# Bits by plain float32 matmuls on the raw head, one V-product block per head, one byte offset for all tiles

## The chip, the cores and the metric

The kernel runs on one core of a Trainium2 chip. The metric is the device time of one execution in microseconds (us), the median of several runs. The profile shows one more execution, instruction by instruction.

## The reference

Attention over 16 heads (2 batches of 8) of 768 tokens by 64, in which a query sees only the keys whose six sign bits against a random projection equal its own, and then two dense layers in a row:

```python
q_bits = (np.einsum('bhsd,dk->bhsk', q, proj) > 0)      # and k_bits; proj is 64 x 6
mask = q_bucket[:, :, :, None] == k_bucket[:, :, None, :]
scores = np.where(mask, scale * np.matmul(q, k.transpose(0, 1, 3, 2)), -1000000000.0)
attn = softmax(scores); x = np.matmul(attn, v)          # 1536 tokens x 512
h = np.maximum(np.maximum(x @ w1, x @ w2), x @ w3) @ w_out
h2 = h @ w_in; g = (h2 + 1)**2 / 4, 0 below -1, h2 above 1
out = g @ w_out2
```

## The kernel before

Two stages follow each other on the tensor engine: the attention of all heads, and the MLP, a long run of 128x512 matmuls. Float32 accuracy comes from pairs of rounded parts (hi, lo, type float32r) and three matmuls per product.

A head has six query tiles of 128 rows, 96 tiles in all. For a tile the tensor engine makes the scores in a bank pair s_ps (four matmuls over 384 keys: L374 with lo and qa, L377 with hi and qb, for each half of the keys), VectorE takes the minimum with a cap and the row's extreme (t_max, L384), ScalarE the exponential (t_exp, L396), the tensor engine transposes the result in six pieces (t_tr, L404, banks t_ps0 and t_ps1), and ScalarE or VectorE copies these into pt (t_out, L413). Three tiles make a group, half a head. Its product with V (g_pv, L422) is six plain float32 matmuls with 64 weight columns; they come in pairs, one into partitions 0 to 63 of the bank u_ps and one into 64 to 127. ScalarE copies the bank out (g_copy, L436 and L439), and SyncE (SP) moves one half beside the other (g_fold: L447 for even heads, one DMA a group; L449 and L450 for odd heads, two). In the text a T is the six transposes of a tile, and a QK its four score matmuls.

The bits of a head enter the score matmul as 12 more rows of qb and hi (rows 64 to 75), as large numbers that push a pair with unequal bits to the cap. bits_mm (L337) makes the projections of half a head by three float32r matmuls with 108 weight columns into pj_ps; the first half is thresholded by VectorE (bits_now, L344), the second by ScalarE and GpSimd (bits_sign L351, bits_rows L359). One DMA (prep_move "kb", L329, hi<-qb) then carries the key's bits from qb to hi. Every QK of that head waits for it.

The raw head r (L272) is scaled and split by GpSimd and moved by further DMAs on SP. All DMAs of the stage stand in SP's one queue, in a fixed order.

That order, and the order on every other engine, comes from a small planner (class Work): each task has an engine, a cost, a due number and what it comes after; the planner replays them at build time and emits each when its turn comes. Its costs are written by hand (for a fold 0.15 us on SP, for a PV group 2.0 us on the tensor engine).

SBUF tiles lie one behind the other, so the byte at which a tile starts within its partition follows from the sizes before it. Counted from a multiple of 256 bytes, before the change ident, x_hl, w and the weight staging start at 0; two small tiles (sums, 48 bytes in two buffers) shift all that follows, so hi, lo, qa, qb, p, pt, vr, and in the MLP wx, hh and g start at 128. The MLP's weights lie in w (five slices of seven) or wx (two of seven).

Of the kernel before, what the change touches and what calls it, by code (L numbers as in the profile page):

```python
# [8 lines left out]
F32 = mybir.dt.float32  # L9
F32R = mybir.dt.float32r  # L10
# [100 lines left out]
def lsh_attention_moe_kernel(  # L111
# [28 lines left out]
    pj_raw = const.tile([128, 108], F32, name="pj_raw")  # L140
    pj_st = const.tile([128, 2, 108], F32R, name="pj_st")
# [107 lines left out]
    def attention(mlp_steps):  # L249
        with ExitStack() as ax, ExitStack() as sx:  # L250
# [4 lines left out]
            pt_p = ax.enter_context(tc.tile_pool(name="pt", bufs=2))  # L255
# [86 lines left out]
            def bits_now(h, half, bank):  # L342
                rows = slice(64, 108)
                nc.vector.tensor_scalar(  # L344
                    out=head[h]["qb"][rows, half * HALF:(half + 1) * HALF], in0=bank[rows, 0:HALF],
                    scalar1=pc_sb[rows, 0:1], scalar2=pc_sb[rows, 1:2], op0=ALU.is_gt, op1=ALU.mult,
                )

            def bits_sign(h, half, bank):
                z = sm_p.tile([128, HALF], F32, tag="z", name="z", bufs=1)  # L350
                nc.scalar.activation(  # L351
                    out=z[64:108], in_=bank[64:108, 0:HALF], func=ACTF.Sign, scale=HUGE, bias=pc_sb[64:108, 2:3]
                )
                head[h]["z", half] = z

            def bits_rows(h, half, eng):
                z = head[h]["z", half]
                rows = slice(64, 108)
                eng.tensor_scalar(  # L359
                    out=head[h]["qb"][rows, half * HALF:(half + 1) * HALF], in0=z[rows],  # L360
                    scalar1=pc_sb[rows, 3:4], scalar2=pc_sb[rows, 3:4], op0=ALU.mult, op1=ALU.add,
                )
# [68 lines left out]
            def g_copy(g):  # L431
                pr, cs = g_cut(g)
                if g % 4 < 2:
                    if g % 4 == 0:
                        pr["u"] = nm_p.tile([128, S], F32, tag="u", name="u")
                    nc.scalar.copy(out=pr["u"][:, cs], in_=u_ps[:, 0:HALF])  # L436
# [83 lines left out]
            pj_split()  # L520
# [35 lines left out]
            def head_tasks(h):
                due = NK * h - 9
                hp, rp = place("prep", NK), place("r", 3)
# [14 lines left out]
                mms, rows = [], []  # L573
                for half in range(2):
                    bp = place("pj", 1)
                    mms.append(task("PE", 0.52, due + 2, bits_mm, h, half, pj_ps, after=[hi] + lo, takes=[bp]))
                    if half == 0:
                        rows.append(task("DVE", 0.72, due + 2, bits_now, h, half, pj_ps, after=[mms[-1]], leaves=[bp]))
                    else:
                        zp = place("z", 1)  # L580
                        sg = task("ACT", 0.69, due + 2, bits_sign, h, half, pj_ps, after=[mms[-1]], takes=[zp], leaves=[bp])
                        rows.append(task("POOL", 0.75, due + 2, bits_rows, h, half, nc.gpsimd, after=[sg], leaves=[zp]))
                kh = task("SP", 0.1, due + 2, prep_move, h, "kh", after=mms + [move["ql"]], lag=3.5)
                kb = task("SP", 0.1, due + 1, prep_move, h, "kb", after=mms + rows + [move["qa"], move["qb"]], lag=2.5)
                ready[h] = [kh, kb, move["qa"], move["ql"]]
# [328 lines left out]
```

## Time and profile before

| | us |
|---|---|
| median of 3 runs (704.96 to 705.01) | 704.96 |
| the profiled execution | 704.98 |
| its span, first to last instruction | 703.2 |
| tensor engine busy | 695.2 |

The profiled execution lies 0.02 us from the median, so sums made on it hold for the median too. 1.8 us lie outside the span. A matmul's row in the profile lasts longer than its turn, since matmuls overlap in the array; the turn is read from the start of one row to the start of the next.

### The profile page before, as it was taken

To read this page: it belongs to the slowest core of one execution; us is meant where nothing else is said; L and a number is where in the kernel's file an instruction comes from. 1 tells how busy PE (TensorE), PEld (TensorE's weight loads), DVE (VectorE), ACT (ScalarE), POOL (GpSimd) and SP (SyncE) were. 2 spreads that over 40 slices of the span, in tenths; PEclk is the share of its full clock that TensorE was granted. 3 is DMA by queue.
4 is the path that set the end of the run, shared out by engine and by line. 5 is a ranking of instruction groups with operands and counts; after the bars stand their busy time and mean duration, and the time that the engine had idled before them with its cause. 6 is when DMAs were issued, how large, how long until landed. Compare 5 with 4: busy or idle time off the path is not lost.

```text
span 703.2 us, 9982 instructions
## 1 busy us (share of the span) xinstructions
PE 695.2 (99%) x3548; PEld 553.9 (79%) x3548; DVE 455.5 (65%) x696; ACT 374.0 (53%) x733; POOL 282.7 (40%) x262
## 2 busy tenths in 40 slices
PE   8999999999999999999999999999999999999998
PEld 6777777777777688888888888888888888888886
DVE  6646555666655486775444355765888888888844
ACT  4788898888888423332321233665544444444430
POOL 3555646647523034442332022444344344344330
PEclk9999999999999999999999999999999999999999
DMA  5655557546511222221111022120111122111004
GB/s 164 162 149 151 132 145 202 139 121 167 132 46 45 95 91 90 90 91 52 56 49 54 31 89 90 47 75 31 60 61 61 60 66 84 61 61 60 31 0 180
DMA packets 25658, 62.78 MB, mean 89 GB/s; under 512 B 4085, under 2 KB 9813, under 8 KB 25609
## 3 DMA queue, kind: packets, MB, share of 16 engines
q1 hardware_dynamic: 25576, 62.15, 29.2%
q8 instruction: 28, 0.46, 0.3%
q14 instruction: 22, 0.17, 0.1%
q0 software_dynamic: 32, 0.00, 0.0%
HBM read 42.07 MB, written 3.19 MB: 64 GB/s over the span
## 4 chain that ended last, share of the span: by engine, by line
PE 97%; DVE 1%; issue 0%; DMA 0%; ACT 0%; DVEq 0%; ACTq 0%
PE b L708 47%; PE b L835 19%; PE u_ps L422 10%; PE t_ps L404 9%; PE s_ps L374 5%; PE s_ps L377 5%; PE pj_ps L337 2%; DMA r<-in_kq 0%; DVE p L384 0%; DVE lo L302 0%; DVE qb L344 0%; DVE qa L331 0%; DVE pt L413 0%; PE pj_ps L469 0%; ACT pt L413 0%
## 5 line engine op out<-in xcount | busy, mean ns | idle before, releaser
L708 PE MATMUL b<-x_hl,w 128*128 128x512 f32 (+1 forms) x900 | 203.1, 382 | 0.0
L708 PEld LDWEIGHTS b<-x_hl,w 128*128 128x128 f32 x900 | 164.0, 188 | 34.2 <-issue 0.6
L384 DVE TENSOR_SCALAR_CACHE_REDUCE p<-s_ps 128x768 f32<-128x768 f32 x96 | 91.1, 955 | 43.7 <-PE s_ps L377 32.4
L735 POOL TENSOR_TENSOR g<-r,g 128x512 fp32r<-128x512 f32 x48 | 62.6, 1306 | 125.6 <-ACT g L734 125.6
L835 PE MATMUL b<-w,g 128*128 128x512 f32 (+1 forms) x438 | 108.4, 392 | 0.0
L219 POOL TENSOR_TENSOR w<-wg,w 128x512 fp32r<-128x512 f32 (+1 forms) x42 | 59.4, 1414 | 96.7 <-ACT w L213 80.8
L835 PEld LDWEIGHTS b<-w,g 128*128 128x128 f32 x438 | 81.9, 189 | 18.7
L396 ACT ACTIVATE p<-p,nm 128x768 f32<-128x768 f32 x96 | 89.8, 937 | 9.0 <-DVE p L384 8.5
L192 DVE SCALAR_TENSOR_TENSOR wg<-wg,wr 128x512 f32<-128x512 f32 (+1 forms) x58 | 66.1, 1140 | 36.2 <-ACT wg L190 35.4
L213 ACT CAST w<-wg 128x512 fp32r<-128x512 f32 (+1 forms) x42 | 25.4, 605 | 115.6 <-DVE wg L205 115.6
L708 PE MATMUL b<-x_hl,wx 128*128 128x512 f32 x360 | 86.1, 395 | 0.0
L404 PEld LDWEIGHTS t_ps<-ident,p 128*128 128x128 f32 x576 | 66.5, 140 | 22.7 <-ACT p L396 11.5
L404 PE MATMUL t_ps<-ident,p 128*128 128x128 f32 x576 | 82.1, 276 | 1.1 <-DVE pt L413 0.9
L708 PEld LDWEIGHTS b<-x_hl,wx 128*128 128x128 f32 x360 | 67.9, 189 | 15.8
L413 ACT COPY pt<-t_ps 128x384 f32<-128x384 f32 x158 | 69.5, 480 | 18.2 <-PE t_ps L404 16.3
L374 PE MATMUL s_ps<-lo,qa 128*128 128x384 f32 x192 | 72.3, 377 | 1.0 <-DVE p L384 0.9
L422 PE MATMUL u_ps<-pt,vr 128*64 128x384 f32 x384 | 69.6, 495 | 0.2 <-ACT pt L413 0.2
L377 PE MATMUL s_ps<-hi,qb 76*128 76x384 f32 x192 | 65.3, 340 | 0.2 <-DVE hi L331 0.2
L815 DVE SCALAR_TENSOR_TENSOR r<-r,b 128x512 f32<-128x512 f32 x48 | 33.0, 687 | 48.2 <-ACT r L814 47.8
L842 DVE TENSOR_TENSOR acc<-b,acc 128x512 f32<-128x512 f32 (+1 forms) x85 | 56.5, 676 | 8.0 <-PE b L835 8.0
L813 ACT ACTIVATE r<-b,half_sb 128x512 f32<-128x512 f32 x48 | 32.9, 686 | 46.1 <-PE b L708 40.8
L197 DVE TENSOR_SCALAR wg<-wg 128x512 int32<-128x512 int32 (+1 forms) x58 | 53.9, 929 | 2.8
(80 smaller groups left out, 847.5 us busy)
## 6 DMA issues: line engine op xcount, KB each, us to landing
wr<-in_w SPq DMA_DIRECT2D x50, 512.0 KB, 3.1
r<-in_kq SPq DMA_DIRECT2D x15, 384.0 KB, 3.9
vr<-in_v SPq DMA_DIRECT2D x16, 192.0 KB
rb<-d SPq DMA_DIRECT2D x16, 192.0 KB, 3.3
wr<-in_w SPq DMA_DIRECT2D x8, 384.0 KB, 2.8
qa<-hi SPq DMA_DIRECT2D x15, 192.0 KB
qb<-hi SPq DMA_DIRECT2D x15, 192.0 KB, 4.0
qa<-lo SPq DMA_DIRECT2D x15, 192.0 KB, 2.7
```

Source lines behind the costliest of these rows:

```text
L192: nc.vector.scalar_tensor_tensor(out=f32(g), in0=f32(g), scalar=TINY_SQ, in1=f32(high), op0=ALU.is_ge, op1=ALU.mult)
L219: nc.gpsimd.tensor_tensor(out=w[:, 1, 0:cols], in0=f32(g2), in1=f32(w[:, 0, 0:cols]), op=ALU.subtract)
L374: nc.tensor.matmul(out=o, lhsT=hd["qa"][:, qs], rhs=hd["lo"][:, ks], start=True, stop=False)
L377: nc.tensor.matmul(out=o, lhsT=hd["qb"][0:76, qs], rhs=hd["hi"][0:76, ks], start=False, stop=True)
L384: nc.vector.tensor_scalar(out=p.rearrange("p (a k) -> p a k", a=2), in0=s_ps[n % 2][:, :, 0:HALF], scalar1=MASKED, scalar2=MASKED, op0=ALU ...
L396: nc.scalar.activation(out=p, in_=p, func=ACTF.Exp, scale=-1.0, bias=tl[n]["nm"], accum_out=pair[h // 2]["sums"][:, c:c + 1],)
L404: nc.tensor.transpose(out=t_ps[half][:, j * 128:(j + 1) * 128], in_=tl[n]["p"][:, kt * 128:(kt + 1) * 128], identity=ident,)
L413: copy(out=grp[g][:, 3 * half:3 * half + 3, r * 128:(r + 1) * 128], in_=t_ps[half][:, 0:HALF].rearrange("p (j q) -> p j q", j=3),)
L422: nc.tensor.matmul(out=u_ps[rows, 0:HALF], lhsT=vr[:, kt, :], rhs=grp[g][:, kt, :], start=(i == 0), stop=(i == 2),)
L708: nc.tensor.matmul(out=outp, lhsT=w_[a], rhs=x_[b_], start=(i == 0 and jj == 0), stop=(i == n - 1 and jj == 2),)
L735: nc.gpsimd.tensor_tensor(out=dst[:, 1, cs], in0=src, in1=f32(dst[:, 0, cs]), op=ALU.subtract)
L835: nc.tensor.matmul(out=pb[:, cs], lhsT=gs[f][:, a, tsl], rhs=wt[:, b_, cs], start=(n == 0), stop=(n == len(terms) - 1),)
```

## The change

The bits of a head are now made from the raw head r, before the split, by one plain float32 matmul per half with 64 weight columns (pj_sc for heads 0 and 1, pj_raw for the others, whose r is scaled in place). The two halves go to the two partition halves of pj_ps, and VectorE thresholds both in one operation (bits_rows, L350 after). The result z is carried by four DMAs (bits_move, L357 after): two into qb, two into hi. For heads 2 to 15 these matmuls stand at the head of a block: bits of head h + 2, then both PV groups of head h, the first into u_ps and the second into pj_ps. So a head has one PV block and not two. pt has four buffers. pj_raw, pj_sc and sums take 256 bytes each, and every tile behind them starts at byte 224 of 256.

```diff
--- before.py
+++ after.py
-    pj_raw = const.tile([128, 108], F32, name="pj_raw")
-    pj_st = const.tile([128, 2, 108], F32R, name="pj_st")
+    pj_raw = const.tile([128, 64], F32, name="pj_raw")
+    pj_sc = const.tile([128, 64], F32, name="pj_sc")
...
-            pt_p = ax.enter_context(tc.tile_pool(name="pt", bufs=2))
+            pt_p = ax.enter_context(tc.tile_pool(name="pt", bufs=4))
...
-                for c0 in (64, 96):
+                for c0 in (0, 32):
                     nc.gpsimd.tensor_scalar(
                         out=pj_raw[:, c0:c0 + 6], in0=pj_raw[:, c0:c0 + 6], scalar1=-1.0, scalar2=0.0, op0=ALU.mult, op1=ALU.add
                     )
-
-            def pj_split():
-                nc.scalar.copy(out=pj_st[:, 0, :], in_=pj_raw)
-                nc.vector.tensor_tensor(out=pj_st[:, 1, :], in0=pj_raw, in1=f32(pj_st[:, 0, :]), op=ALU.subtract)
+                nc.gpsimd.tensor_scalar(
+                    out=pj_sc, in0=pj_raw, scalar1=sc_sb, scalar2=0.0, op0=ALU.mult, op1=ALU.add
+                )
...
-            def bits_mm(h, half, bank):
-                hd = head[h]
-                cs = slice(half * HALF, (half + 1) * HALF)
-                for i, (part, name) in enumerate(((0, "hi"), (1, "hi"), (0, "lo"))):
-                    nc.tensor.matmul(
-                        out=bank[0:108, 0:HALF], lhsT=pj_st[:, part, :], rhs=hd[name][:, cs],
-                        start=(i == 0), stop=(i == 2),
+            def bits_mm(h, half, bank, rows=DOWN):
+                nc.tensor.matmul(
+                    out=bank[rows, 0:HALF], lhsT=pj_sc if h < 2 else pj_raw,
+                    rhs=head[h]["r"][:, half * HALF:(half + 1) * HALF], start=True, stop=True,
+                )
...
+            def bits_both(h):
+                bits_mm(h, 0, pj_ps, DOWN)
+                bits_mm(h, 1, pj_ps, UP)
+
+            def bits_rows(h):
+                z = sm_p.tile([128, HALF], F32R, tag="z", name="z", bufs=2)
+                nc.vector.tensor_scalar(
+                    out=z, in0=pj_ps[:, 0:HALF], scalar1=pc_sb[:, 0:1], scalar2=pc_sb[:, 1:2], op0=ALU.is_gt, op1=ALU.mult
+                )
+                head[h]["z"] = z
+
+            def bits_move(h, to, first):
+                for half, at in ((0, first + 64), (1, first)):
+                    nc.sync.dma_start(
+                        out=f32(head[h][to][64:76, half * HALF:(half + 1) * HALF]), in_=f32(head[h]["z"][at:at + 12])
                     )
...
-                    pair[h // 2] = dict(sums=nm_p.tile([128, 2 * NK], F32, tag="sums", name="sums"))
+                    pair[h // 2] = dict(sums=nm_p.tile([128, 64], F32, tag="sums", name="sums")[:, 0:2 * NK])
...
-            def g_pv(g, first, count):
+            def g_pv(g, first, count, bank=u_ps):
...
-                            out=u_ps[rows, 0:HALF], lhsT=vr[:, kt, :], rhs=grp[g][:, kt, :],
+                            out=bank[rows, 0:HALF], lhsT=vr[:, kt, :], rhs=grp[g][:, kt, :],
                             start=(i == 0), stop=(i == 2),
                         )
+
+            def block(h, bits):
+                if bits:
+                    bits_both(bits)
+                    bits_rows(bits)
+                    work.at["DVE"] = work.at.get("DVE", 0.0) + 0.69
+                g_pv(2 * h, 0, 3)
+                if h < NH - 1:
+                    g_pv(2 * h + 1, 0, 3, pj_ps)
...
-                    nc.scalar.copy(out=pr["uo", g], in_=u_ps[:, 0:HALF])
+                    nc.scalar.copy(out=pr["uo", g], in_=bank[:, 0:HALF])
...
+            def bits_tasks(h, rows, zp, due):
+                qa, qb, ql, kh = moves[h]
+                kb = [
+                    task("SP", 0.2, due, bits_move, h, to, first, after=[rows, qa, qb], leaves=[zp], lag=2.5)
+                    for to, first in (("qb", 0), ("hi", 32))
+                ]
+                ready[h] = [kh, *kb, qa, ql]
...
+            def block_tasks(h, outs):
+                up, pj_, bits = place("u_ps", 1), place("pj", 1), h + 2 if h + 2 < NH else 0
...
+                blk = task(
+                    "PE", 0.3 + 1.95 * (1 + both) + (0.66 if bits else 0.0), 6 * h + (8.4 if both else 5.4), block, h, bits,
...
+                if bits:
+                    bits_tasks(bits, blk, zp, 6 * bits - 3)
...
```

The other lines give the planner these tasks, make r's buffer wait for the bits, and let the bits of head h + 2 be prepared two heads ahead. The kernel's order changes so at three places.

**The tensor engine around a PV group of head 1, before.** lo_177 and hi_176 are the split of head 1, whose scores go on here; hi_317 and lo_318 are the split of head 3, whose second bits half it is; pt_408 is the first group of head 1 and vr_209 its V:

```order
L374 MATMUL s_ps1_114<-lo_177,qa_178 128x384
L377 MATMUL s_ps1_114<-hi_176,qb_179 128x384
L374 MATMUL s_ps1_114<-lo_177,qa_178 128x384
L377 MATMUL s_ps1_114<-hi_176,qb_179 128x384
L337 MATMUL pj_ps_85<-hi_317,pj_st_77 108x384 x2
L337 MATMUL pj_ps_85<-lo_318,pj_st_77 108x384
L422 MATMUL u_ps_84<-pt_408,vr_209 64x384 x6
L404 MATMUL t_ps0_115<-ident_83,p_440 128x128 x3
L404 MATMUL t_ps1_116<-ident_83,p_440 128x128 x3
```

**The block of head 1, after.** lo_255 and hi_254 are the split of head 2, r_221 is the raw head 3, pt_375 and pt_455 are the two groups of head 1 and vr_180 its V:

```order
L371 MATMUL s_ps0_113<-lo_255,qa_256 128x384
L374 MATMUL s_ps0_113<-hi_254,qb_257 128x384
L401 MATMUL t_ps0_115<-ident_83,p_482 128x128 x3
L401 MATMUL t_ps1_116<-ident_83,p_482 128x128 x3
L333 MATMUL pj_ps_85<-r_221,pj_raw_76 64x384 x2
L419 MATMUL u_ps_84<-pt_375,vr_180 64x384 x6
L419 MATMUL pj_ps_85<-pt_455,vr_180 64x384 x6
L401 MATMUL t_ps0_115<-ident_83,p_506 128x128 x3
L401 MATMUL t_ps1_116<-ident_83,p_506 128x128 x3
```

The six float32r matmuls of a head's bits, in two places of three, have become two plain ones at the head of the block, and the second group of V now follows the first, into pj_ps.

**The tensor engine from the end of that block to the first score of head 3 (lo_305), after:**

```order
L371 MATMUL s_ps1_114<-lo_255,qa_256 128x384
L374 MATMUL s_ps1_114<-hi_254,qb_257 128x384
L371 MATMUL s_ps1_114<-lo_255,qa_256 128x384
L374 MATMUL s_ps1_114<-hi_254,qb_257 128x384
L401 MATMUL t_ps0_115<-ident_83,p_526 128x128 x3
L401 MATMUL t_ps1_116<-ident_83,p_526 128x128 x3
L401 MATMUL t_ps0_115<-ident_83,p_560 128x128 x3
L401 MATMUL t_ps1_116<-ident_83,p_560 128x128 x3
L371 MATMUL s_ps0_113<-lo_305,qa_306 128x384
```

Between the block of head 1 and the first QK of head 3 there are a T (the rows of p_506 above), a QK and two Ts. It is so behind every block of an odd head h from 1 to 13, before head h + 2. Behind the blocks of even heads there are three Ts and three QKs.

**SP before**, around the folds of head 1 (uo_486 and uo_578 hold its two groups; hi_317 and qb_320 belong to head 3):

```order
L449 DMA uc_366<-uo_486 64x384
L450 DMA u_357<-uo_486 64x384
L329 DMA qa_464<-lo_463 64x768
L272 DMA r_502<-in_kq 128x768
L329 DMA hi_317<-qb_320 12x768
L478 DMA d_573<-rt_570 12x128
L279 DMA vr_580<-in_v 128x384
L449 DMA uc_366<-uo_578 64x384
L450 DMA u_357<-uo_578 64x384
L484 DMA rb_603<-d_573 64x768 x2
```

**SP after**, around the block of head 1 (z_543 holds the bits of head 3, whose hi is hi_304 and whose qb is qb_307; uo_571 and uo_578 hold the two PV groups of head 1):

```order
L485 DMA d_533<-rt_531 12x128
L328 DMA qa_494<-lo_493 64x768
L491 DMA rb_563<-d_533 64x768 x2
L357 DMA qb_307<-z_543 12x384 x2
L456 DMA uc_410<-uo_571 64x384
L457 DMA u_403<-uo_571 64x384
L456 DMA uc_410<-uo_578 64x384
L457 DMA u_403<-uo_578 64x384
L357 DMA hi_304<-z_543 12x384 x2
```

The bits' way into hi, one DMA of 12 rows before, is two of half the length after (x2), and they stand behind the four folds of uo_571 and uo_578, the last two of which carry what the block's last matmuls make. At the blocks of even heads one fold stands there.

## Rows read from the trace of the kernel before

**Rows 1.** Stretch, us; busy PE, PEld, DVE, ACT, POOL (counts); PE clock, DMA share, GB/s.

```profile
20.00:220.00 200.00, 200.00 (x1312) 151.61 (x1311) 118.06 (x242) 169.87 (x374) 107.16 (x122) 1.00 0.52 137
236.00:703.00 467.00, 463.85 (x2055) 380.59 (x2053) 318.72 (x414) 184.14 (x319) 165.56 (x122) 1.00 0.20 68
```

**Rows 2.** Timeline of the tensor engine: start, us, line, tiles, count [idle before].

```profile
101.27 0.82 PE L404 MATMUL t_ps<-ident,p 128*128 128x128 f32 x6
101.84 0.42 PE L374 MATMUL s_ps<-lo,qa 128*128 128x384 f32 x1
102.10 0.34 PE L377 MATMUL s_ps<-hi,qb 76*128 76x384 f32 x1
102.28 0.34 PE L374 MATMUL s_ps<-lo,qa 128*128 128x384 f32 x1
...
102.64 0.52 PE L337 MATMUL pj_ps<-hi,pj_st 128*108 128x384 f32 x2
...
103.17 0.82 PE L404 MATMUL t_ps<-ident,p 128*128 128x128 f32 x6
103.92 2.16 PE L422 MATMUL u_ps<-pt,vr 128*64 128x384 f32 x12
106.00 0.87 PE L404 MATMUL t_ps<-ident,p 128*128 128x128 f32 x6
106.63 0.59 PE L337 MATMUL pj_ps<-hi,pj_st 128*108 128x384 f32 x2
```

**Rows 3.** Timeline, narrow windows inside that PV block: two matmul rows each.

```profile
105.26 0.49 PE L422 MATMUL u_ps<-pt,vr 128*64 128x384 f32 x2
...
105.58 0.49 PE L422 MATMUL u_ps<-pt,vr 128*64 128x384 f32 x2
```

**Rows 4.** Timeline of the tensor engine in the MLP's first layer.

```profile
269.64 6.97 PE L708 MATMUL b<-x_hl,w 128*128 128x512 f32 x30
276.45 16.91 PE L708 MATMUL b<-x_hl,wx 128*128 128x512 f32 x72
293.19 7.01 PE L708 MATMUL b<-x_hl,w 128*128 128x512 f32 x30
```

**Rows 5.** Groups by line and form, MLP: count | busy us, mean ns of one.

```profile
L835 PE MATMUL b<-w,g 128*128 128x512 f32 x426 | 107.0, 395 | 0.0
L708 PE MATMUL b<-x_hl,wx 128*128 128x512 f32 x360 | 86.1, 395 | 0.0
L708 PE MATMUL b<-hh,w 128*128 128x512 f32 x162 | 38.7, 395 | 0.0
```

**Rows 6.** Groups by line, attention, ScalarE and VectorE.

```profile
L396 ACT ACTIVATE p<-p,nm 128x768 f32<-128x768 f32 x84 | 78.6, 937 | 3.7 <-DVE p L384 3.2
...
L384 DVE TENSOR_SCALAR_CACHE_REDUCE p<-s_ps 128x768 f32<-128x768 f32 x83 | 78.8, 955 | 42.4 <-PE s_ps L377 31.5 <-PE t_ps L404 10.0
...
L344 DVE TENSOR_SCALAR qb<-pj_ps,pc_sb 44x384 fp32r<-44x384 f32 x12 | 8.2, 686 | 0.7 <-issue 0.3
```

**Rows 7.** Timeline of ScalarE behind the same PV block.

```profile
106.17 0.48 ACT L436 COPY u<-u_ps 128x384 f32<-128x384 f32 x1 [0.69 <-PE u_ps L422]
```

**Rows 8.** Timeline of SP: start and time of DMA issues.

```profile
121.23 0.46 SPq L449 DMA_DIRECT2D uc<-uo  x1
121.73 0.59 SPq L450 DMA_DIRECT2D u<-uo  x1
123.13 0.80 SPq L329 DMA_DIRECT2D hi<-qb  x1
```

**Rows 9.** DMA issues by tile: count, KB each, median us from issue to landing.

```profile
u<-uo SPq DMA_DIRECT2D x15, 96.0 KB, 2.1
```

**Rows 10.** Timeline of the start: VectorE and the tensor engine.

```profile
8.22 0.69 DVE L344 TENSOR_SCALAR qb<-pj_ps,pc_sb 44x384 fp32r<-44x384 f32 x1
...
9.42 0.44 PE L377 MATMUL s_ps<-hi,qb 76*128 76x384 f32 x1 [0.17 <-DVE hi L331]
...
13.14 0.69 DVE L344 TENSOR_SCALAR qb<-pj_ps,pc_sb 44x384 fp32r<-44x384 f32 x1
```

More of the change, by code (lines that the diff above doesn't have):

```diff
@@ L342, in bits_now @@
[L342 to L362, printed above, removed]
+            def bits_mm(h, half, bank, rows=DOWN):
[3 more added lines that the diff above has]
+                )
@@ L432, in g_copy @@
                 pr, cs = g_cut(g)
+                bank = (u_ps, pj_ps)[g % 2]
                 if g % 4 < 2:
@@ L435, in g_copy @@
                         pr["u"] = nm_p.tile([128, S], F32, tag="u", name="u")
[L436 removed]
+                    nc.scalar.copy(out=pr["u"][:, cs], in_=bank[:, 0:HALF])
                 else:
                     pr["uo", g] = nm_p.tile([128, HALF], F32, tag="uo", name="uo")
[L439 removed]
+                    nc.scalar.copy(out=pr["uo", g], in_=bank[:, 0:HALF])
                 grp.pop(g)
@@ L552, in attention @@
             ready, vready, h_place, v_place = {0: []}, {}, {0: place("prep", NK)}, {}
+            scaled, moves, r_place = {}, {}, {}
             raw_s["prep"].free.pop()
@@ L572, in head_tasks @@
                     move[x] = task("SP", 0.1, due, prep_move, h, x, after=after, lag=5)
[L573 to L585, printed above, removed]
+                kh = task("SP", 0.1, due + 2, prep_move, h, "kh", after=[move["ql"]], lag=3.5)
+                scaled[h] = ld if h == 1 else sc
+                moves[h], r_place[h] = [move["qa"], move["qb"], move["ql"], kh], rp
+                if h == 1:
+                    bp, zp = place("pj", 1), place("z", 2)
+                    mm = task("PE", 0.66, due + 1, bits_both, h, takes=[bp], leaves=[rp])
+                    bits_tasks(h, task("DVE", 0.69, due + 1, bits_rows, h, after=[mm], takes=[zp], leaves=[bp]), zp, due + 1)
+            def bits_tasks(h, rows, zp, due):
[5 more added lines that the diff above has]
+                ready[h] = [kh, *kb, qa, ql]
             def v_tasks(h):
                 due = NK * h - 2
-                vr = place("vr", 2)
+                vr = place("vr", 1)
                 v_place[h] = vr
@@ L618, in tile_tasks, with group_tasks @@
                 return outs
-            def group_tasks(g, outs):
+            def block_tasks(h, outs):
+                up, pj_, bits = place("u_ps", 1), place("pj", 1), h + 2 if h + 2 < NH else 0
+                zp = place("z", 2)
+                both = h < NH - 1
+                blk = task(
+                    "PE", 0.3 + 1.95 * (1 + both) + (0.66 if bits else 0.0), 6 * h + (8.4 if both else 5.4), block, h, bits,
+                    after=outs + [vready[h]] + ([scaled[bits]] if bits else []),
+                    takes=[up] + ([pj_] if both else []) + ([zp] if bits else []),
+                    leaves=[pt_p_[2 * h], v_place[h]] + ([pt_p_[2 * h + 1]] if both else []) + ([r_place[bits]] if bits else []),
+                )
+                if bits:
+                    bits_tasks(bits, blk, zp, 6 * bits - 3)
+                group_tasks(2 * h, blk, up)
+                if both:
+                    group_tasks(2 * h + 1, blk, pj_)
+            def group_tasks(g, last, up):
                 h = g // 2
-                up = place("u_ps", 1)
-                last = None
-                for i in range(1):
-                    last = task("PE", 2.0, 3 * g + 5.4, g_pv, g, 0, 3, after=outs + [vready[h], last], takes=[up] if i == 0 else [], leaves=[pt_p_[g], v_place[h]])
                 if g % 4 == 0:
@@ L630, in group_tasks @@
                 takes = [uo] if g % 4 > 1 else [u_p[h // 2]] if g % 4 == 0 else []
-                co = task("ACT", 0.38, 3 * g + 1.5, g_copy, g, after=[last], takes=takes, leaves=[up])
+                co = task("ACT", 0.38, 6 * h + 4.5 + g % 2, g_copy, g, after=[last], takes=takes, leaves=[up])
                 adds[g] = task(
-                    "SP", 0.15, 3 * g + 2.5, g_fold, g, after=[co] + ([adds[g - 2]] if g % 4 > 1 else []),
+                    "SP", 0.15, 6 * h + 5.5 + g % 2, g_fold, g, after=[co] + ([adds[g - 2]] if g % 4 > 1 else []),
                     takes=[uc_p[h // 2]] if g % 4 == 0 else [], leaves=[uo] if g % 4 > 1 else [], lag=3.5,
@@ L883 @@
     vt = v.reshape(B * H, NK, 128, D).transpose(0, 2, 1, 3)
-    pj = np.zeros((128, 108), proj.dtype)
-    for rows, c0 in ((slice(0, 64), 96), (slice(64, 128), 64)):
+    pj = np.zeros((128, 64), proj.dtype)
+    for rows, c0 in ((slice(0, 64), 32), (slice(64, 128), 0)):
         pj[rows, c0:c0 + 6] = proj
@@ L890 @@
     past = -np.nextafter(edge, np.float32(1))
-    for rows, first, top in ((64, edge, 1.0), (70, past, 1.0), (96, past, BIG), (102, edge, BIG)):
-        pc[rows:rows + 6] = [first, top, -0.5 if first > 0 else 0.5, 0.5 * top]
+    for rows, first, top in ((0, edge, 1.0), (6, past, 1.0), (32, past, BIG), (38, edge, BIG)):
+        pc[rows:rows + 6] = pc[rows + 64:rows + 70] = [first, top, -0.5 if first > 0 else 0.5, 0.5 * top]
     mw = {n: np.asarray(a) for n, a in inputs.items() if n.startswith("moe")}
```

22 lines of the change are left out of this document (13 added, 9 removed).

## The prediction

> **What bounds the kernel now.** I read the stretches first: from 20 to 220 us, the attention, the tensor engine is busy 200.00 of 200 us, and in the MLP 463.85 of 467, both at a granted clock of 1.00, its upper level of 2.4 GHz [rows 1]. ScalarE follows in the attention with 85%, VectorE with 59%. A busy tensor engine need not be a fast one, so the next view is its timeline, read from start to start. In the attention it runs without a hole: six transposes (T) take 0.57 us, the four matmuls of a QK 0.80 [rows 2], so a tile costs 1.37. A block of one V group takes 2.08, from 103.92 to 106.00. Each half of a head's bits takes 0.53, from 102.64 to 103.17. Hence a microsecond that leaves the tensor engine leaves the kernel, and a microsecond for which it waits is added; the other engines matter only where they make it wait.
>
> **Bits.** Six float32r matmuls per head cost 2 x 0.53 = 1.06 us. After the change there are two plain float32 matmuls with 64 weight columns and 384 moved columns, one for each partition half: the shape of one V pair, of which a group has three. The profile shows a plain matmul as two rows, so a pair has four. Inside a V block two rows start together, and the next two 0.32 later [rows 3]: two such steps make 0.65 for the pair. This is the price if the pair is streamed like V's, and I see no reason why not: 0.41 less per head, for the 14 heads 2 to 15 that stand in blocks, 5.7 us. The Trainium skill, FP8 and Floating Point Precision, section TensorE Precision Notes, gives true float32 four passes through the array, which speaks against one plain matmul in place of three: four passes would be 0.71 a half, and the sum 10.6 us worse than by the rows. The rows decide otherwise: two matmuls in opposite column halves run side by side.
>
> **Blocks.** Twelve rows of V would be six steps of 0.32, 1.93 us; the block takes 2.08, so 0.15 goes to its ends. The T ahead of it takes 0.75 where others take 0.57, but there the first matmul of a QK behind a T takes 0.26 and not 0.18 [rows 2], which is paid anyway: 0.10 more. The T behind it takes 0.63: 0.06. A block's ends cost 0.30. There were 31 blocks (groups 0 to 30), there will be 16: 15 x 0.30 = 4.5 us less.
>
> **Offsets.** In the first MLP layer x_hl starts at byte 0 of 256, w at 0 too and wx at 128. Thirty matmuls with w take 6.81 us, 227.0 ns each; the next 72 with wx take 16.74, 232.5 ns [rows 4]. So unequal offsets cost 5.5 ns each. Unequal are w with g, wx with x_hl and hh with w, 426 + 360 + 162 = 948 matmuls [rows 5]; 948 x 5.5 = 5.2 us less, if equal offsets run at 227.0 at byte 224 too, which no row shows. The attention's tiles had equal offsets already, but for ident (0) against p (128) in 576 transposes. No row has these at equal offsets: between nothing and the full 5.5 ns (3.2 us) I take the price scaled to 128 columns, 1.4 ns, 0.8 us.
>
> **The start.** Bits of head 1 now stand ahead of the first QK, wait for pj_ps, which VectorE reads until 8.91 in the old run, and push back the matmul that started at 9.42 [rows 10]; 0.65 plus a block's ends give at most 1.4 us. In return VectorE drops the 0.69 at 13.14 that stood between the first two tiles, and pj_st ahead of everything. Between 0 and 1.4 I take 0.3.
>
> **The new wait.** What the change adds is in SP's order. The bits of head h + 2 reach hi by two DMAs that stand, at blocks of odd heads, behind four folds, the last two of which wait for the block's end. I walk this block from its first matmul, 0. The tensor engine makes 14 steps, 0.32 each with 0.05 more at the first: the last V step for u_ps starts at 2.3, for pj_ps at 4.24, the next T at 4.66. VectorE thresholds from 0.9 to 1.6 (0.69 as before [rows 6]); the tile that waits there gets its 0.96 until 2.6, ScalarE's 0.94 for it until 3.6, and only then comes the copy of u_ps, 0.48, until about 4.1. The copy of pj_ps starts 0.59 behind the last V step, as 106.17 follows 105.58 [rows 3, 7], and ends at 5.3. SP needs 0.50 for the first fold of a pair and about 0.6 for the second [rows 8]: the first pair goes from 4.1 to 5.2, the second from 5.3 to 6.4, and the first hi move is issued then. A small SBUF move lands 2.1 us after its issue [rows 9]: 8.5. The tensor engine, meanwhile, does a T (0.63 behind the block), a QK (0.80), a T ahead of another (0.65, since it pays the 0.08 itself), a T (0.57) and the first matmul of the QK (0.26): 4.66 + 2.91 = 7.6 for the first matmul that reads hi. It waits 0.9, and since the second hi move is issued 0.46 to 0.80 later [rows 8] while its reader follows after 0.35, another 0.1 to 0.5. That is 1.0 to 1.4; rb's two DMAs and the qb moves ahead in the queue can add up to 0.9. I take 1.3 at each of the 7 odd blocks with bits: 9.1 us more. Queued behind on SP are r and v of later heads, wanted a head's time (some 13 us) later.
>
> At even blocks only one fold stands ahead: hi moves go out near 4.8 and land near 7.0, and the tensor engine wants them after three Ts and three QKs, near 9.0. This cover of 2 us is why I cost them at nothing.
>
> **Costed at nothing.** ScalarE loses bits_sign and GpSimd bits_rows, neither of which is waited for. VectorE's threshold stays one operation. Three DMAs more per head fit in SP's queue. Weight loads at byte 224 are slower at most where DMA is busy 20% of the time. While a block runs ScalarE gets at most two exponentials; its slack of 15% is nearly used up there, but the walk shows only one wait for it, under the wait for hi.
>
> **Sum.** 704.98 - 5.7 - 4.5 - 5.2 - 0.8 + 9.1 + 0.3 = 698.2. The profiled run equals the median to 0.02, so this is also the forecast for the median.
>
> **Rivals.**
> - *No wait for hi.* If moves of 12 half rows are issued and land faster, or SP's folds are done earlier, ScalarE still holds the second T behind the block, since it copies u_ps and pj_ps first: some 0.45, its copy time [rows 7], at 7 places, 3.2 us. Then 692.3, and 689.1 without even that. For it: the cover misses by only 0.9. Against: the chain of copy, two folds and landing begins at the block's end, and no step of it is long.
> - *The wait is longer.* With 0.80 for every 12-row issue and rb ahead it is 2.6: 18.2 us, 707.3, slower than before. It decides from (5.7 + 4.5 + 5.2 + 0.8 - 0.3) / 7 = 2.27 us per odd block on. For it: hi<-qb took 0.80 for its 12 rows [rows 8]. Against: its rows were twice as long, and rb's landing is wanted earlier than the block's end.
> - *The offset does nothing.* Rows 4 and 5 have only 0 and 128; if the 5.5 ns go with the place of wx and not with its byte, the 6.0 us stay and the time is 704.2. Against: w, the fast one with x_hl, has with g and hh the same mean of 395 ns as wx with x_hl [rows 5]. The Trainium skill, SBUF — State Buffer, section Specifications, knows lines of 16 bytes, and 0, 128 and 224 all begin one, so by this page no offset differs and the time would be this 704.2; rows 4 disagree with that for 0 and 128. Worse, byte 224 could be slow for all: with the 5.5 ns on the other 1,100 MLP matmuls too, 710.3.
>
> **How the numbers follow.** Forecast 0.45, no wait 0.25, longer wait 0.12, offset without effect 0.12, offset slow 0.06. The forecast's own range, waits of 0.9 to 1.9, is 695.4 to 702.4. For 8 in 10 I go from 690.5, inside the first rival with most of it kept, to 707.0, which leaves out the upper halves of the second and the last. A change of 0.2%, 1.4 us, is about what a measurement of this kernel can tell from none. Faster by more: 0.45 + 0.25 and a third of the offset case, 0.74; within it 0.08, half the offset case and the edge of the long wait; slower 0.18.
>
> **What would show it.** Bits ahead of a V block in 0.65 to 0.7; a block of 24 V rows in about 4.0; wx and w at one pace near 227 ns, and g with w too; T at 108 ns per piece or less; and a hole ahead of the hi matmul of heads 3, 5, ... 15, released by the DMA from z, of 1 to 1.4 us, with none at even heads. I am wrong if that hole is missing or over 2.3, if byte 224 has a pace of its own, or if ScalarE's copies hold the Ts in the rest of the head.

## The result, and the profile after

The changed kernel takes 715.42 us (median of 4 runs, 713.72 to 716.56) where the kernel before takes 704.96: a ratio of 1.0146, 95% interval 1.0127 to 1.0165. It is 10.5 us slower. The forecast was 698.2, its range ended at 707.0, and the sign was wrong. The profiled run took 716.56, with a span of 714.8; holes and clock below are those of profiled runs, times are medians.

The stretches come first, as in [rows 1]: busy time of PE, PEld, DVE, ACT and POOL, then the clock, the DMA share and GB/s.

```profile
20.00:220.00 200.00, 185.99 (x1166) 136.07 (x1167) 113.36 (x233) 139.86 (x314) 91.62 (x101) 0.97 0.54 135
254.00:714.00 460.00, 457.67 (x2058) 380.38 (x2056) 317.99 (x414) 184.10 (x320) 165.28 (x122) 1.00 0.21 69
```

The attention has lost its full tensor engine, 185.99 of 200 us, and its full clock, 0.97. The MLP has neither trouble. Its groups, to be laid beside [rows 5], and its first-layer timeline, beside [rows 4]:

```profile
L856 PE MATMUL b<-w,g 128*128 128x512 f32 x426 | 104.5, 389 | 0.0
L729 PE MATMUL b<-x_hl,wx 128*128 128x512 f32 x360 | 84.0, 389 | 0.0
L729 PE MATMUL b<-hh,w 128*128 128x512 f32 x162 | 37.7, 389 | 0.0
```

```profile
253.59 41.85 PE L729 MATMUL b<-x_hl,w 128*128 128x512 f32 x216
295.28 16.48 PE L729 MATMUL b<-x_hl,wx 128*128 128x512 f32 x72
311.60 18.75 PE L729 MATMUL b<-x_hl,w 128*128 128x512 f32 x82
```

All three groups fell from 395 to 389 ns. Seventy-two matmuls with wx take 311.60 - 295.28 = 16.32 us, 226.7 ns each, where they took 16.74. The MLP, from its first matmul (253.59) to the end of the span (714.79), takes 461.2 us; before, it began so:

```profile
234.82 1.43 PE L708 MATMUL b<-x_hl,w 128*128 128x512 f32 x5
```

That left it 468.4 of the 703.2. So the MLP gave 7.2 us, and the attention took 18.8 more: its end moved from 234.82 to 253.59.

What the tensor engine waited for (total, times, longest):

```profile
PE s_ps L374 <- DMA hi<-z: 11.1, 9, 4.7
PE t_ps L401 <- ACT pt L410: 1.9, 8, 0.2
PE pj_ps L333 <- DVE qb L339: 1.7, 1, 1.7
PE s_ps L371 <- DVE p L381: 1.5, 2, 1.0
PE s_ps L374 <- issue: 1.3, 1, 1.3
```

The first line is the wait that was forecast, at the hi matmul that opens a head. Here is one, the block of head 1 with the bits of head 3: the tensor engine, VectorE's threshold, ScalarE's two copies, then SP (SyncE).

```profile
40.47 0.87 PE L333 MATMUL pj_ps<-r,pj_raw 128*64 128x384 f32 x4
41.16 2.10 PE L419 MATMUL u_ps<-pt,vr 128*64 128x384 f32 x12
43.10 2.10 PE L419 MATMUL pj_ps<-pt,vr 128*64 128x384 f32 x12
45.13 0.87 PE L401 MATMUL t_ps<-ident,p 128*128 128x128 f32 x6
...
48.30 0.42 PE L371 MATMUL s_ps<-lo,qa 128*128 128x384 f32 x1
50.24 0.42 PE L374 MATMUL s_ps<-hi,qb 76*128 76x384 f32 x1 [1.52 <-DMA hi<-z]
```

```profile
41.44 0.68 DVE L350 TENSOR_SCALAR z<-pj_ps,pc_sb 128x384 fp32r<-128x384 f32 x1 [0.63 <-PE pj_ps L333]
```

```profile
44.02 0.46 ACT L446 COPY uo<-u_ps 128x384 f32<-128x384 f32 x1
45.25 0.48 ACT L446 COPY uo<-pj_ps 128x384 f32<-128x384 f32 x1 [0.78 <-PE pj_ps L419]
```

```profile
42.66 1.11 SPq L491 DMA_DIRECT2D rb<-d  x2
43.87 1.60 SPq L357 DMA_DIRECT2D qb<-z  x2
45.57 0.53 SPq L456 DMA_DIRECT2D uc<-uo  x1
46.15 0.59 SPq L457 DMA_DIRECT2D u<-uo  x1
46.79 0.59 SPq L456 DMA_DIRECT2D uc<-uo  x1
47.42 0.60 SPq L457 DMA_DIRECT2D u<-uo  x1
48.06 1.59 SPq L357 DMA_DIRECT2D hi<-z  x2
```

The walk of the prediction can be laid over it, with 0 at 40.47. The bits take 0.69, each V group 1.94 to 2.03, the threshold ends at 1.65, the copies at 4.0 and 5.3: all as walked. SP is not: rb (the reciprocals of the softmax sums, brought back from a DRAM tile by two DMAs) holds it until 43.77, 1.65 us past the end of the threshold, the two qb moves take 1.60, and it comes to hi at 7.6 instead of 6.4. The matmul that needs hi could start at 48.30 + 0.26, which is 8.1, and starts at 9.8: a hole of 1.68. In what follows a hole is this: the time by which the first hi matmul of a head starts later than 0.26 behind its lo matmul.

The longest hole, 4.9 us, is at head 7:

```profile
104.09 1.75 SPq L178 DMA_DIRECT2D wr<-in_w  x2
105.94 1.61 SPq L357 DMA_DIRECT2D qb<-z  x2
...
109.43 0.60 SPq L457 DMA_DIRECT2D u<-uo  x1
112.26 2.19 SPq L357 DMA_DIRECT2D hi<-z  x2
```

```profile
SPq L357 <- DMA wr<-in_w: 2.8, 2, 2.2
```

SP is free at 110.03 but issues the first hi move at 112.26: its wait is for one of two 512 KB weight loads issued eight DMAs ahead of it.

The last new thing is the clock:

```profile
80.00:84.00 4.00, 3.31 (x12) 2.93 (x13) 0.97 (x2) 0.97 (x3) 1.15 (x3) 0.59 0.52 157
...
114.00:122.00 8.00, 6.97 (x25) 5.26 (x27) 2.73 (x6) 2.91 (x6) 5.80 (x7) 0.57 0.40 106
...
176.00:180.00 4.00, 3.86 (x16) 3.71 (x15) 1.48 (x3) 1.88 (x4) 1.52 (x3) 0.57 0.46 147
```

Behind the holes of heads 5, 7 and 11 the granted clock stands at its lower level, 1.2 GHz, for some microseconds (the means mix in full speed at the edges): 4 x 0.41 + 8 x 0.43 + 4 x 0.43 = 6.8 us lost, if the tensor engine had work all that time.

### The profile page after: what moved, and what is told of

Same layout as the page of the kernel before. It is cut to its first block, busy times and chain, and to the rows that moved or that the text cites. A ratio compares the mean times of both kernels' runs of the same rounds, so it can differ in the third digit from the quotient of the medians.

```text
span 714.8 us, 9973 instructions
## 1 busy us (share of the span) xinstructions
PE 691.8 (97%) x3516; PEld 549.2 (77%) x3516; DVE 460.5 (64%) x710; ACT 356.3 (50%) x702; POOL 273.7 (38%) x248
## 4 chain that ended last, share of the span: by engine, by line
PE 88%; DMA 4%; DVE 3%; SPq 2%; ACT 1%; issue 1%; DVEq 0%; ACTq 0%
PE b L729 46%; PE b L856 18%; PE t_ps L401 6%; PE u_ps L419 4%; PE s_ps L374 4%; PE pj_ps L419 4%; PE s_ps L371 4%; DMA hi<-z 2%; PE pj_ps L333 2%; DVE p L381 1%; DMA wr<-in_w 1%; ACT pt L410 1%; SPq L357 1%; SPq L457 1%; DVE lo L301 0%
## 5 line engine op out<-in xcount | busy, mean ns | idle before, releaser
L856 PE MATMUL b<-w,g 128*128 128x512 f32 (+1 forms) x438 | 106.0, 387 | 0.0
L410 ACT COPY pt<-t_ps 128x384 f32<-128x384 f32 x143 | 63.9, 479 | 40.7 <-PE t_ps L401 39.6
L729 PE MATMUL b<-x_hl,wx 128*128 128x512 f32 x360 | 84.0, 389 | 0.0
L374 PE MATMUL s_ps<-hi,qb 76*128 76x384 f32 x192 | 69.5, 362 | 12.8 <-DMA hi<-z 11.1
L401 PEld LDWEIGHTS t_ps<-ident,p 128*128 128x128 f32 x576 | 68.2, 143 | 17.5 <-issue 4.2
L371 PE MATMUL s_ps<-lo,qa 128*128 128x384 f32 x192 | 74.9, 390 | 1.7 <-DVE p L381 1.5
L205 DVE SCALAR_TENSOR_TENSOR wg<-wr,wg 128x512 int32<-128x512 int32 (+1 forms) x58 | 52.6, 907 | 0.9
```

Of the source, the lines that this page charges most:

```text
L371: nc.tensor.matmul(out=o, lhsT=hd["qa"][:, qs], rhs=hd["lo"][:, ks], start=True, stop=False)
L374: nc.tensor.matmul(out=o, lhsT=hd["qb"][0:76, qs], rhs=hd["hi"][0:76, ks], start=False, stop=True)
L401: nc.tensor.transpose(out=t_ps[half][:, j * 128:(j + 1) * 128], in_=tl[n]["p"][:, kt * 128:(kt + 1) * 128], identity=ident,)
L410: copy(out=grp[g][:, 3 * half:3 * half + 3, r * 128:(r + 1) * 128], in_=t_ps[half][:, 0:HALF].rearrange("p (j q) -> p j q", j=3),)
L729: nc.tensor.matmul(out=outp, lhsT=w_[a], rhs=x_[b_], start=(i == 0 and jj == 0), stop=(i == n - 1 and jj == 2),)
L856: nc.tensor.matmul(out=pb[:, cs], lhsT=gs[f][:, a, tsl], rhs=wt[:, b_, cs], start=(n == 0), stop=(n == len(terms) - 1),)
```

## The experiments

Each time stands beside the kernel before on the same chip (704.97 to 705.02), with its ratio and interval.

**Offsets alone.** In the kernel before, only the sums tile is padded:

```diff
- sums=nm_p.tile([128, 2 * NK], F32, tag="sums", name="sums"))
+ sums=nm_p.tile([128, 64], F32, tag="sums", name="sums")[:, 0:2 * NK])
```

> The kernel before with only its sums tile made 64 columns wide, so that nearly all SBUF tiles of matmul operands begin at byte 0 of 256, ident and p among them; the order of no engine changes. If equal offsets are what sped the MLP up in the changed kernel, 948 matmuls go from 395 to 389 ns in duration and the MLP from 468.4 to 461.2 us, at byte 0 as at byte 224: 697.8, with nothing from the transposes (their pace was 109 ns in both kernels). If the transposes had gained 1.4 ns each, 697.0. If the MLP's 7.2 us came from something else in the change: 705.

Measured: 698.20, ratio 0.9902 (0.9887 to 0.9917). The groups of [rows 5] again:

```profile
L835 PE MATMUL b<-w,g 128*128 128x512 f32 x426 | 104.5, 389 | 0.0
L708 PE MATMUL b<-x_hl,wx 128*128 128x512 f32 x360 | 84.0, 389 | 0.0
L708 PE MATMUL b<-hh,w 128*128 128x512 f32 x162 | 37.7, 389 | 0.0
```

So the offsets are the MLP's gain but for 0.1 us, at byte 0 as at 224 (461.3 here, 461.2 there); the attention ends at 235.09, no earlier than before.

**The moves ahead of the folds.**

```diff
- bits_tasks(bits, blk, zp, 6 * bits - 3)
+ bits_tasks(bits, blk, zp, 6 * bits - 9)
```

> The changed kernel with one number changed, the due time of the bit moves in a block, so that SyncE issues the two moves into hi right behind those into qb and ahead of the folds; TensorE's order is the same. Theory A (the wait for hi is the chain of copy, folds and moves on SyncE, and the low clock follows from the holes it leaves): the moves take 0.73 to 0.78 each on SyncE, so the last is issued 1.6 + 4 x 0.76 = 4.6 us behind the block's first matmul and lands near 6.8, before TensorE asks at 7.6. The holes at heads 3 to 15 go (11.1 us of waits for hi<-z), the granted clock stays at 1.00 (about 6.8 us more), so the attention ends near 235.5 and the time is 696 to 699. Theory B (the clock falls because long blocks of plain float32 matmuls are themselves light work for TensorE): the holes go, but the clock still falls to 0.5 in places, 702 to 706. Theory C (ScalarE, which copies both banks late, is what holds, and the wait only changes its name): the waits move to the T matmuls for pt, 708 or more.

Measured: 713.72, ratio 1.0116 (1.0099 to 1.0133). Only 1.7 us came back, less than the spread of the runs of either kernel, and none of the three theories holds: the waits did not move to T. The holes are 11.7 us instead of 13.3: two are left at odd heads (0.7 at head 5, and 6.7 at head 7, longer than before), and there are new ones at even heads. At head 6 z was ready at 85.2, and SP did this, GpSimd that:

```profile
87.85 0.48 SPq L328 DMA_DIRECT2D qa<-hi  x1
88.42 0.55 SPq L328 DMA_DIRECT2D qb<-hi  x1
89.91 0.46 SPq L328 DMA_DIRECT2D qa<-lo  x1
90.46 1.61 SPq L357 DMA_DIRECT2D qb<-z  x2
```

```profile
82.11 1.02 POOL L466 TENSOR_TENSOR u<-u,uc 128x384 f32<-128x384 f32 x1 [10.72 <-DMA u<-uo]
...
87.00 0.82 POOL L311 CAST hi<-r 128x768 fp32r<-128x768 f32 x1
```

GpSimd stood 10.72 us for the folds, which the merged block issues late, before it prepared the next head; SP waited for that head's hi, and the moves of z, ready for 5 us, stood behind. The Trainium skill, DMA: Bandwidth & Descriptors, section Anatomy of one DMA — SWDGE (gpsimd) path, says that a semaphore wait happens on the issuing sequencer and not in the DMA engines. That section is about DMAs that GpSimd issues; these rows show the same for SP, and that the wait holds whatever SP has behind it.

**Weight loads elsewhere, holes filled.**

```diff
- w_load, 2, after=[exps[40]]
+ w_load, 2, after=[exps[44]]
```

> The changed kernel with the two 512 KB weight loads that SyncE issues inside the attention moved from just ahead of the block of head 5 to after head 8's qa and qb moves. Theory: the hole of 5.15 us at head 7 came from them, since a move into hi waited on SyncE for a weight load eight DMAs ahead of it (2.2 us) and was late besides; it should be 1.3 to 2.2 us like those of heads 3, 5 and 11, the stretch of low clock behind it shorter (6.8 us before), and the time 3 to 6 us less: 709 to 712. Rival: the loads only move the hole to another head and the time stays at 714 to 716.

Measured: 714.98, ratio 1.0140 (1.0125 to 1.0155), no gain: head 7's hole fell from 4.9 to 2.6, while heads 9 and 11 grew to 2.3 and 3.7 (13.7 in all). The rival holds.

```diff
+ for _ in range(FILL.get(h, 0)):   # first lo and hi of a head
+     nc.tensor.matmul(out=u_ps[:, 384:512], lhsT=warm[:, 0:128], rhs=warm[:, 0:128], ...)
```

> The changed kernel with small bf16 matmuls on the zero tile (128 columns, 8 to 64 of them, sized to the holes seen) between the first lo and the first hi matmul of heads 3, 5, ... 15. SyncE's order and the landing of hi stay as they are. Theory A (the clock falls because TensorE stands idle in the hole): the holes are as long as before but full, the granted clock stays near 1.00 and the 13.6 us at half clock give back about 6.8: 707 to 710. Theory B (the clock falls for the block's own work): still stretches at 0.5, 714 to 716. If the holes' length is itself due to the low clock, it would be less than 707.

Measured: 714.17, ratio 1.0134 (1.0108 to 1.0161). By its time it would be theory B. The windows say otherwise:

```profile
78.00:84.00 6.00, 4.74 (x51) 4.06 (x50) 1.71 (x4) 2.33 (x6) 1.81 (x2) 1.00 0.50 112
110.00:122.00 12.00, 10.52 (x107) 7.98 (x107) 5.25 (x11) 5.23 (x11) 5.16 (x6) 1.00 0.48 109
172.00:180.00 8.00, 7.51 (x61) 5.72 (x61) 3.75 (x9) 4.88 (x11) 3.24 (x4) 1.00 0.49 129
206.00:212.00 6.00, 6.00 (x29) 4.25 (x31) 3.10 (x6) 2.83 (x6) 3.66 (x5) 0.72 0.44 127
```

At the three places of the low clock the same blocks now run at 1.00, although they wait as long. It fell elsewhere, behind a hole of head 13 that was hardly filled and behind an idle stretch of 2 us at the start: 3.4 us lost instead of 6.8. The holes summed to 15.3 here, 2 more than in the changed kernel, so the gain does not show in the time of this run, the slowest of four (717.34). The other three show a mean granted clock of 1.000, where the changed kernel has 0.988 to 0.993, and still take 712.54 to 714.26. So filling the holes keeps the clock up, but that alone buys little: the 6.8 us cannot simply be added back.

**SP's order cleared.** The moves ahead of the folds, the weight loads off the block, rb and GpSimd's additions of the folds planned later, and the bits of head 1 behind its hi and lo:

```diff
- pair_store, p_, after=[cp], takes=[dp], leaves=[rp], lag=2.5)
+ pair_store, p_, after=[cp], takes=[dp], leaves=[rp], lag=6)
- takes=[uc_p[h // 2]] if g % 4 == 0 else [], leaves=[uo] if g % 4 > 1 else [], lag=3.5,
+ takes=[uc_p[h // 2]] if g % 4 == 0 else [], leaves=[uo] if g % 4 > 1 else [], lag=10,
```

> TensorE's order of the changed kernel kept (but for the bits of head 1, which go behind the first QK), and SyncE's and GpSimd's orders mended by the planner's numbers alone: the bit moves ahead of the folds, rb behind them, the weight loads off the odd block, and GpSimd's additions of the folds behind the preparation of the next head instead of ahead of it. Theory A (from thresholds to the first use there are only 6.4 to 7.5 us, where the kernel before had 10 to 12 over most heads; four moves at 0.76 and a landing of about 2 need 5.2 of them, so every wait that SyncE has ahead of the moves, up to 5.3 us in the run with the moves ahead of the folds, becomes a hole): with SyncE free the moves are issued at once, the waits for hi<-z fall from 11 us to under 2, the clock stays at 1.00, the start is about 2 us earlier: 694 to 699. Theory B (the lead is too short whatever the queue does): holes of 1 to 2 us stay at half the heads, 702 to 710.

Measured: 721.28, ratio 1.0232 (1.0216 to 1.0247), slower still and outside both ranges. Yet the picture is clear: at all odd heads SP issues the first move within 0.1 us of the threshold and no hole is left; at heads 4 to 14 it issues 5.1 to 6.6 us late, and the holes are 14.8 us. Head 6, SP and GpSimd:

```profile
80.14 0.54 SPq L272 DMA_DIRECT2D r<-in_kq  x1
...
87.80 0.49 SPq L328 DMA_DIRECT2D qa<-hi  x1
...
90.42 1.62 SPq L357 DMA_DIRECT2D qb<-z  x2
```

```profile
86.06 0.83 POOL L293 TENSOR_SCALAR r<-r 64x768 f32<-64x768 f32 x1 [16.43 <-DMA r<-in_kq]
```

The load of the next r can only go out behind the block, whose bits matmuls are now the last reader of its buffer. A third buffer for r tests that:

```diff
- raw_p.tile([128, S], F32, tag="r", name="r")
+ raw_p.tile([128, S], F32, tag="r", name="r", bufs=3)
```

> The run with the cleared queue, with a third buffer for r (the raw head), paid for by one buffer less of z. In the cleared queue the odd heads lost their holes and the even ones kept 1.2 to 3.9 us: there the moves of z stand on SyncE behind the qa and qb moves of the next head, these wait for GpSimd's hi, and GpSimd for a load of r that SyncE issues only behind the block, because the bits matmuls of the block are the last reader of that buffer. Theory A (it is this buffer): with three buffers the load goes out a head earlier, qb<-z is issued within 2 us of the threshold at even heads too, no hole over 0.5, clock 1.00: the 14 us of waits and 11.9 of clock go from 721.3, 694 to 698, TensorE's order being that of the changed kernel. Theory B (the lead of the merged block is too short in itself): holes of over 1 us at even heads, above 705.

Measured: 712.75, ratio 1.0113 (1.0090 to 1.0136). Theory A falls in part: the holes went from 14.8 to 8.8, no further, and those of over 1 us at even heads that theory B forecast stay. SP is still 3.4 to 6.3 us late at even heads from 4 on. At head 6 r is no longer what it waits for; its longest wait there is for the landing of qa<-lo, in a burst of rb, r and three moves behind the block:

```profile
SPq L328 <- DMA qa<-lo: 6.4, 1, 6.4
```

Each wait cleared at the head of SP's queue let the next one show.

**More lead.** What the runs so far share is the lead: the time from the threshold's end to where the first hi matmul would start, 6.1 to 7.8 us. The kernel before had 6.5 to 12.8, with a median of 10.9, and a single move to make. So the bits were taken out of the merged block and put between tiles, earlier:

```diff
- if h == 1:
+ if True:
      bp, zp = place("pj", 1), place("z", 2)
-     mm = task("PE", 0.66, due + 1, bits_both, h, takes=[bp], leaves=[rp])
+     mm = task("PE", 0.66, due + 3 if h > 1 else due + 1, bits_both, h, after=[scaled[h]], ...)
- up, pj_, bits = place("u_ps", 1), place("pj", 1), h + 2 if h + 2 < NH else 0
+ up, pj_, bits = place("u_ps", 1), place("pj", 1), 0
```

> The changed kernel with the two bits matmuls of a head taken out of the block and put between two tiles, as early as the planner likes (some 4 to 8 tiles ahead of the block's place); the V block stays merged. It costs a second pair of ends, 0.30 x 14 = 4.2 us. Theory A (the lead): from threshold to use there are then 12 us or more, the holes go (13.3 us by the table of heads), so does the low clock (6.8 us): 715.4 - 13.3 - 6.8 + 4.2 = 699.5, between 697 and 703. Theory B (SyncE is overloaded by 15 x 3 more DMAs, whatever the lead): holes stay, above 708.

Measured: 699.87, ratio 0.9930 (0.9915 to 0.9945), theory A to 0.4 us, which is partly luck: 2.9 us of holes and 3.4 of low clock stay, which its sum had at nothing, so some 6 us of other terms were off the other way. The lead is 12.3 to 22.6 us; SP is late by up to 12.0, and only that one (head 12) is seen by the tensor engine:

```profile
PE s_ps L374 <- DMA hi<-z: 2.7, 1, 2.7
```

Then each half of the change alone, both with equal offsets, to be compared with 698.2:

> The kernel before with equal offsets and only the V groups of a head merged into one block over two banks, with the old bits of three float32r matmuls between tiles. Against 698.2: 15 pairs of ends of 0.30 less, 693.7; plus 0.40 for the second T behind a block, which waits for ScalarE's copy, at up to 15 blocks, 6.0: 699.7 if all of them wait. If the merged block's late folds are what delays GpSimd and through it SyncE (the chain seen at head 6), holes appear here too and it is above 702. Forecast 697.

The diff joins the two V groups of a head into one task over u_ps and pj_ps, as the change does. Measured: 699.93, ratio 0.9928 (0.9914 to 0.9943). Merging alone loses 1.7 us. A block of 24 rows takes 4.02 where two of 12 take 2.09 each, but the trace lists 5.6 us of waits of the tensor engine, 3.7 of them for VectorE's copies and maxima and 1.1 for one late hi (head 10), where the run with equal offsets alone lists 2.0 of these kinds.

> The plain float32 bits and the equal offsets of the changed kernel, but V in two blocks of one group as in the kernel before, and the bits between tiles with one head less of advance in the tasks. Against 698.2 of the kernel before with equal offsets: 0.41 less for each of 14 heads, 692.5, if nothing waits; plus the waits for hi, if the four moves of 0.76 each are what makes it late (theory B), up to 13 us, 705. Theory A (short lead of the merged block): no holes, 691.5 to 694.

The diff keeps V as before and the bits task between tiles. Measured: 695.75, ratio 0.9868 (0.9851 to 0.9884). No hole, but 2.4 us gained against 698.2 instead of 5.7: a pair of bits standing alone takes 0.80, and 0.15 more from its neighbours, where it takes 0.70 in front of V.

**Bits in front of the first V block.** Hence V in two blocks, with the bits of head h + 2 leading the first of head h; and a second kernel, in which one number makes them lead the second V block, three tiles later:

```diff
+ bits = h + 2 if g % 2 == 0 and h + 2 < NH else 0    # bits_lead_second: g % 2 == 1
  last = task("PE", 2.0 + (0.66 if bits else 0.0), 3 * g + 5.4, block, g, bits, ...)
```

> Plain float32 bits and equal offsets, V in two blocks of one group as before, but the bits of head h + 2 lead the first V block of head h instead of standing alone: the lead from threshold to use grows by three tiles against the merged block, some 12 us. Alone the bits cost 0.80 and 0.15 of their neighbours in the run with bits only; in front of V they cost 0.70, with ends that V pays anyway. So 0.25 less for each of 14 heads against 695.75: 692.2, between 691 and 694 if nothing waits for hi. With holes as in the merged block: above 700.

Measured: 692.76, ratio 0.9829 (0.9815 to 0.9842): the fastest of all, 12.2 us below the kernel before. 7.2 of it is the MLP's, the rest the attention's, which ends at 229.84. The lead is 10.7 to 14.4, no hole and no low clock is left:

```profile
20.00:220.00 200.00, 199.98 (x1314) 145.04 (x1313) 115.25 (x245) 162.80 (x368) 96.93 (x108) 1.00 0.56 140
```

> The run in which the bits lead the first V block of a head, with one number changed: they lead the second V block, which stands at about the tile where the changed kernel has its merged block. TensorE does the same work, V stays in two blocks. Theory A (the lead from threshold to use is what decides, merged V or not): the lead falls from some 12 to 6.5 to 9 us, holes for hi<-z come back at part of the heads, some 4 to 11 us with low clock behind the longer ones: 697 to 708. Theory B (the burst behind the merged block is what made the moves late, not the lead): no holes, 692 to 694.

Measured: 709.72, ratio 1.0057 (1.0041 to 1.0074). That is 1.7 above theory A's range, but what theory A names is there: the lead falls to 4.5 to 7.9, the holes come back (9.6 us, most of it in four waits for hi), and the clock falls in three places (5.1 us):

```profile
PE s_ps L374 <- DMA hi<-z: 8.7, 4, 2.6
```

The tensor engine's work is the same in both and V is merged in neither. Three tiles of lead are worth 17 us. They do not come alone: SP also reaches the moves later, up to 4.0 us behind the threshold where the faster kernel has at most 2.9, and the holes over 2 us stand where a lead of 4.7 to 5.6 meets a delay of 3.7 to 4.0. All of it in one table; holes and leads of heads 2 to 15 counted from start to start on the tensor engine, low clock as half the time that it lasted (part of it falls into a hole, 2.2 us of it with the moves ahead of the folds):

| kernel | lead, us | holes, us | lost to low clock, us | time, us |
|---|---|---|---|---|
| before | 6.5 to 12.8 | 0 | 0 | 704.96 |
| changed | 6.4 to 7.5 | 13.3 | 6.8 | 715.42 |
| moves ahead of folds | 6.4 to 7.8 | 11.7 | 6.8 | 713.72 |
| weight loads later | 6.4 to 7.5 | 13.7 | 5.1 | 714.98 |
| holes filled | 6.4 to 7.5 | 15.3 | 3.4 | 714.17 |
| SP cleared | 6.1 to 7.5 | 14.8 | 11.9 | 721.28 |
| SP cleared, third r | 6.1 to 7.5 | 8.8 | 6.8 | 712.75 |
| bits lead second V | 4.5 to 7.9 | 9.6 | 5.1 | 709.72 |
| bits apart, V merged | 12.3 to 22.6 | 2.9 | 3.4 | 699.87 |
| bits apart, V as before | 12.2 to 29.2 | 0 | 0 | 695.75 |
| bits lead first V | 10.7 to 14.4 | 0 | 0 | 692.76 |

## Why the prediction was wrong, step by step

- **Bits and blocks**: right as work. Counted from start to start against the same steps in runs without holes, the attention's matmuls need 9.5 us less; the two terms said 10.2. But merging V as such did not pay: alone it ended 1.7 us slower. Two plain matmuls in opposite halves run side by side (0.69 for four rows), which bears out the rows. The Trainium skill, FP8 and Floating Point Precision, section TensorE Precision Notes, gives true float32 four passes; the prediction priced them with one matmul behind the other, 2 x 0.71, and that does not show here. The page itself is not refuted: four passes in both at once would take about 0.7, an estimate from that page and the 0.18 from start to start of a float32r matmul of 384 columns [rows 2], and 0.69 was measured.
- **Offsets**: right in kind, 7.2 instead of 5.2. The unequal pairs gained 5.7 to 5.8 ns each, about as priced; the other 1.7 came from equal pairs that stand among them (wx with g from 228.8 to 226.6 ns, for one). Byte 224 has no pace of its own. The transposes gained nothing of their 0.8.
- **The start**: the step said "Between 0 and 1.4 I take 0.3". The first QK begins at 9.86 instead of 8.03: 1.8 us, since the bits of head 1 wait 1.7 for VectorE.
- **The new wait**: this is the step that failed, by its size. It said "I take 1.3 at each of the 7 odd blocks with bits: 9.1 us more". The mechanism was right, but waits at the hi matmuls cost 15.3 us and the T behind the block 2.2, together 17.5: the rival *The wait is longer* had 18.2. The walk gave "up to 0.9" to everything that stands ahead of the folds on SP; the two qb moves alone take 1.6, and SP came to them 0 to 3.7 us after the threshold. Its waits for GpSimd, for rb's round trip and for the weight loads were left out, and "Three DMAs more per head fit in SP's queue", put at nothing, did not hold for moves that are wanted this soon.
- **Even blocks**: "This cover of 2 us is why I cost them at nothing" held here by luck. The hole of head 4 costs 0.5 in the changed kernel, and holes of even heads sum to 14.8 once SP's order moved.
- **What was missing**: the low clock behind the holes, 6.8 us. No row of the kernel before showed anything but 1.00, and no bound was kept for it. The Trainium skill, TensorE: Matmul & The Clock Gate, section HAM oscillation — how this bites in real kernels, tells how a wait for a DMA sends the clock down, so that the work behind it starts slow. The trace agrees, with the lower level behind holes of 1.9, 4.9 and 1.3 us; two of these waits are shorter than those the page tells of.

The sum for the attention: -9.5 + 17.5 + 6.8 + 1.8, and 1.9 more behind the transposes of the sums, where the next tile waits for VectorE, make 18.5; measured 18.8. This is a sum for one run, not what each term would give back alone, as the filled holes show.

That it is the place of the bits, and so their lead against SP's queue, is shown: two kernels that differ in it alone differ by 17 us. How the 17 split between the shorter lead and SP's greater delay is not shown. That the clock falls because the engine stands idle is supported by the filled holes, not proven; against the other theory, the work of long blocks, speaks that with V merged alone the clock stayed at 1.00. Why merged V blocks alone lose 1.7 us was read from the trace only and not tried further.

## What to carry to other kernels

When work is moved later to save an engine time, measure how long its result now has until its first reader, and set against it the whole in-order queue that carries it, with every entry ahead that can wait; an average of short issues says nothing. Here it paid to keep the cheap form of the work and give it back its lead: bits in front of V cost 0.70 at either block, and three tiles of lead were worth 17 us. And price a hole of the tensor engine above its length, since the clock may fall behind it.

## What the runs showed of the hardware

- Matmuls whose two operands begin at different bytes of 256 (0 and 128) take 232.5 ns from start to start (float32r, 512 columns, kernel before), 226.7 with both at 0 (equal offsets alone) or both at 224 (changed kernel).
- A move of 12 half rows between SBUF tiles holds SP for 0.71 to 0.80 us in most cases, one of 64 whole rows for 0.46 to 0.60 (changed kernel).
- The clock did not fall behind every hole of a length: those of 1.9 us (head 5) and 1.3 (head 11) were followed by 1.2 GHz, those of 1.7 (head 3) and 1.4 (head 15) were not, nor one of 2.6 (head 7) in the run with later weight loads. Runs with such holes also spread more: 713.72 to 716.56, where the kernel before has 704.96 to 705.01.
